# Memory attention and an eight-expert layer in one kernel: first weight splits one step earlier, one count later, and late pairs of blocks with a half-full second block

## The chip, the cores and the metric

The kernel runs on one core of one Trainium2 chip. A core has a matrix engine (TensorE, PE in the profile; its weight loads are shown as PEld), a vector engine (VectorE, DVE), a scalar engine (ScalarE, ACT), a general engine (GpSimd, POOL) and a queue engine that issues DMAs (SyncE, SP). Each engine takes its instructions in the order of the program; between engines, semaphores make one wait for another. Matrix products land in PSUM, which has eight banks of 128 x 512 float32; everything else lies in SBUF.

The metric is the device time of one execution in microseconds. Lower is better. The profile is one execution, taken by the hardware profiler; its span runs from the first to the last instruction.

## What is computed

Attention over 32 memory slots for 8 batches of 8 heads, and then a layer of eight experts in which each token goes to one expert:

```python
a = softmax(phi)                      # over 32 memory slots, phi: 8 x 8 x 576 x 32
k_m = einsum('bhsm,bhsd->bhmd', a, k) # memories, 32 x 64 per head
v_m = einsum('bhsm,bhsd->bhmd', a, v)
attn = softmax(q @ k_m^T / 8)
x = (attn @ v_m)                      # heads put side by side: 4608 tokens x 512
logits = x @ w_gate                   # 8 experts
e_idx = argmax(logits, axis=1)
for e in range(8):
    mask = e_idx == e
    h = relu(x[mask] @ w1[e])         # 512 -> 1024
    ye = h @ w2[e]                    # 1024 -> 512
    out[mask] = gate_w[mask] * sigmoid(x[mask] @ w_output_gate[:, e]) * ye
```

All inputs are float32. On the inputs that are drawn, the experts get 576, 576, 0, 0, 576, 1152, 1152 and 576 tokens, worked out from the reference. In blocks of 128 rows, 576 is four full blocks and one of 64 rows, and 1152 is nine full blocks.

## The kernel before

**Stages.** The first stage is attention for four pairs of batches (`bp`). For each, chunks of k and v and the softmax of phi become memories (`memory`), and then 5 steps of 1024 queries run through `scores`, `shift`, `expo`, `divide`, `back` and `values`; the rows x go to a DRAM table `xs` with their two gate factors behind them. After each pair of batches, `rank` finds each token's expert and its rank within the expert. The second stage is the expert layer, in slots of three blocks of 128 rows (a triple), two blocks (a pair), or one (a single), all of one expert. It starts before attention is over.

**Slots.** There are 5 early triples, which are filled from the first two and then three pairs of batches (`route_early`, lists `idx_a` and `idx_b`), and, once all tokens are known (`route_late`, list `idx_l`), 5 late triples, 4 pairs and up to 22 singles. Triples and pairs always run; the singles stand behind branches and run only if some are used. `route_late` forms the number of blocks left per expert, takes triples off it, makes a pair of two that remain, and a single of one.

**A slot.** Weights come as 8 tiles of 128 x 1024 float32 per slot (`Stream`): `fetch` issues the DMA on SP, `split` makes two parts of a tile, the rounded part with a cast on ACT (L564) and the rest with a subtraction on DVE (L565), in a tile `whl` with both. x and h are split the same way, and a product takes three matmuls, high by high, low by high and high by low (`PASS`). In `several`, the first four tiles (units u of 0 to 3) give h transposed: per unit two halves of 12 matmuls each (L1176), then ReLU into `hh` on ACT (L1181) and the remainder into `hl` on DVE (L1182). The second four tiles give y per block k: per unit and block two chunks f of three matmuls of 512 columns (L1198), with 128 x 128 of `hh` or `hl` as the loaded weights. `finish_y` scales y with the gate on ACT (L1155) and scatters the rows with an indirect DMA from POOL. In the last slot of a stream the turns (u, k) are sorted by k.

**x for the next slot.** While a slot's y runs, `nxt` prepares the next slot's x in four parts c of 0 to 3 (`turn_x`), at the turns that `TURN` lists. For early slots PE transposes (L1041). For the late ones that are gathered in quarters, DVE transposes `xg` into `xt` (L1035), ACT rounds it to `xh` (L1043) and DVE subtracts to `xl` (L1044); each such slot also has four small copies `gx` on ACT (L1031).

**Order.** The program is written out by Python generators. `ORDER` is the list of pieces of one attention step; each piece is one tick. "W" is the piece that splits the first two weight tiles, at step `START` = 17; the expert layer starts at piece "S" of that step. From there, `hook` runs at each half unit and each turn: it advances attention by three pieces and routing by two. `hold(n)` lets n ticks pass between a piece of routing that one engine does and the piece of another that needs it. `counts` is one small matmul that adds the counts `ohc` over the partitions (L278). `MEM` is the same kind of list for `memory`.

```python
def hold(n):
    if "open" not in env: return
    end = clock[0] + n
    while clock[0] < end: yield
```

The functions that the diff touches are printed here with the line numbers of the profile.

## Time and profile before

| | us |
|---|---|
| median of 3 runs | 578.09 (577.61 to 582.82) |
| the profiled execution | 577.36 |
| its span | 575.6 |
| PE busy | 529.1 (92%) |
| DVE busy | 356.1 (62%) |
| ACT busy | 280.4 (49%) |
| POOL busy | 229.2 (40%) |

A row of the timeline gives the start and the duration in microseconds, the engine, the line, the operation, what is written from what, shapes and count, and in brackets the time that the engine sat idle before it and what ended that. A row of a table of windows gives the stretch, its length, the busy time of each engine, the mean granted PE clock as a share of full speed, the share of the DMA engines that was busy, and GB/s. Rows of the timeline that are merged cover several instructions; matmuls overlap, so a row's duration is longer than the distance from one to the next.

### The profile page before, as it was taken

Reading aid. Unit: us, or ns where it says so; the run is one execution under the profiler, and the core shown is the slowest. Engines: PE = TensorE matmul, PEld = TensorE weight load, DVE = VectorE, ACT = ScalarE, POOL = GpSimd, SP = SyncE. Lnnn points to the kernel's source line nnn. Section 1 sums busy time; section 2 is a strip of 40 time slices with the busy share of each in tenths; the row PEclk is TensorE's granted clock in tenths of the full one; section 3 lists DMA queues with packets and bytes.
Section 4 is the critical chain, followed back from the end, with each engine's and each line's share of the span. In section 5 each row is a group of like instructions: output and inputs, shape, how many; then the busy total and the mean of one; then the engine's idle time right before and its main releaser. Section 6 shows DMA issues by size and latency. Waiting matters only on the chain. (4 is left out here: it accounts for less than half of the span.)

```text
span 575.6 us, 10886 instructions
## 1 busy us (share of the span) xinstructions
PE 529.1 (92%) x4031; PEld 455.6 (79%) x4031; DVE 356.1 (62%) x736; ACT 280.4 (49%) x496; POOL 229.2 (40%) x253
## 2 busy tenths in 40 slices
PE   3688886789899999999999999999999999999993
PEld 2455554478689799898998989898998989899893
DVE  4485979767765659996443555646465555676610
ACT  3475655454254456453434545445454445656510
POOL 2242575831166034312471735547170604553011
PEclk9987879989899999999999999999999999999998
DMA  8999999975367659756564665656465655687000
GB/s 308 413 401 391 382 376 356 308 301 168 116 197 245 209 173 308 246 155 183 161 200 145 204 177 180 184 171 176 139 202 168 179 172 181 198 264 223 7 28 32
DMA packets 42238, 124.14 MB, mean 216 GB/s; under 512 B 10368, under 2 KB 10432, under 8 KB 41792
## 3 DMA queue, kind: packets, MB, share of 16 engines
q1 hardware_dynamic: 35136, 102.71, 54.7%
q0 software_dynamic: 7040, 20.65, 10.4%
q8 instruction: 33, 0.54, 0.4%
q14 instruction: 29, 0.24, 0.1%
HBM read 102.99 MB, written 20.87 MB: 215 GB/s over the span
## 5 line engine op out<-in xcount | busy, mean ns | idle before, releaser
L1176 PE MATMUL bps<-xh,whl 128*128 128x384 f32 (+1 forms) x896 | 213.6, 322 | 0.1
L1198 PE MATMUL bps<-whl,hh 128*128 128x512 f32 x608 | 197.7, 396 | 0.0
L565 DVE TENSOR_TENSOR whl<-w,whl 128x1024 fp32r<-128x1024 f32 x112 | 136.8, 1228 | 68.5 <-ACT whl L564 68.5
L1176 PEld LDWEIGHTS bps<-xh,whl 128*128 128x128 f32 x896 | 156.9, 190 | 1.9 <-issue 0.6
L1176 PE MATMUL bps<-xl,whl 128*128 128x384 f32 (+1 forms) x448 | 143.8, 321 | 0.0
L1198 PEld LDWEIGHTS bps<-whl,hh 128*128 128x128 f32 x608 | 114.7, 189 | 26.1 <-issue 2.5
L1198 PE MATMUL bps<-whl,hl 128*128 128x512 f32 x304 | 119.0, 391 | 0.0
L564 ACT CAST whl<-w 128x1024 fp32r<-128x1024 f32 x112 | 116.4, 1046 | 0.0
L519 POOL DMA_INDIRECT xg<-xs,idx_ql x80 | 90.2, 1127 | 25.2 <-issue 24.3
L1181 ACT ACTIVATE hh<-bps 128x384 fp32r<-128x384 f32 (+1 forms) x96 | 48.9, 510 | 96.9 <-PE bps L1176 96.7
L1182 DVE SCALAR_TENSOR_TENSOR hl<-bps,hh 128x384 fp32r<-128x384 f32 (+1 forms) x96 | 55.1, 577 | 52.1 <-ACT hh L1181 52.1
L1176 PEld LDWEIGHTS bps<-xl,whl 128*128 128x128 f32 x448 | 85.1, 190 | 0.5
L1156 POOL DMA_INDIRECT out<-y,idx_ol x23 | 24.9, 1081 | 127.1 <-ACT y L1155 101.4
L1198 PEld LDWEIGHTS bps<-whl,hl 128*128 128x128 f32 x304 | 57.5, 189 | 10.8
L838 POOL TENSOR_TENSOR ea<-ea,mx 128x512 f32<-128x512 f32 (+1 forms) x20 | 19.2, 961 | 49.8 <-DVE mx L836 45.4
L1043 ACT CAST xh<-xt 128x384 fp32r<-128x384 f32 (+1 forms) x32 | 14.7, 460 | 37.9 <-DVE xt L1035 37.9
L873 ACT COPY xo<-bpd 128x576 f32<-128x576 f32 x36 | 22.6, 640 | 21.3 <-PE bpd L871 12.7
L956 POOL TENSOR_SCALAR Aw<-iota_row,row 128x128 bf16<-128x128 bf16 x36 | 26.8, 759 | 12.4 <-DVE row L946 12.4
L871 PE MATMUL bpd<-ve_b,aT 64*128 64x144 f32 (+1 forms) x320 | 28.5, 327 | 2.4 <-DVE ea L833 2.4
L1044 DVE TENSOR_TENSOR xl<-xt,xh 128x384 fp32r<-128x384 f32 (+1 forms) x32 | 15.8, 492 | 24.1 <-ACT xh L1043 24.1
L1155 ACT ACTIVATE y<-bps,gx 128x512 f32<-128x512 f32 x20 | 13.4, 687 | 30.4 <-PE bps L1198 13.9
L871 PEld LDWEIGHTS bpd<-ve_b,aT 64*128 64x128 f32 (+1 forms) x320 | 21.7, 196 | 8.1 <-issue 3.5
(248 smaller groups left out, 471.6 us busy)
## 6 DMA issues: line engine op xcount, KB each, us to landing
w<-wall SPq DMA_DIRECT2D x112, 512.0 KB, 3.9
kvt<-kv SPq DMA_DIRECT2D x32, 512.0 KB, 7.5
xs<-xo SPq DMA_DIRECT2D x16, 576.0 KB, 5.8
qt<-qT SPq DMA_DIRECT2D x16, 512.0 KB, 9.1
ph<-phiT SPq DMA_DIRECT2D x3, 1152.0 KB, 12.1
kv<-kv SPq DMA_DIRECT2D x4, 512.0 KB, 9.0
xg<-xs,idx_ql POOLq DMA_INDIRECT x80, 4.2
ph<-phiT SPq DMA_DIRECT2D x4, 288.0 KB, 3.2
```

Of the source, the lines that this page charges most:

```text
L519: G.indirect_dma_start(out=z["xg"][:, k, XQ * b:XQ * b + XQ], out_offset=None, in_=xs[0:z["rows"]].rearrange("t (a q) -> (t a) q", a=4), i ...
L564: A.copy(hl[:, 0], w[:])
L565: V.tensor_tensor(hl[:, 1], w[:], hl[:, 0].bitcast(F32), ALU.subtract)
L838: G.tensor_tensor(eav, eav, mx[:, 0:n].unsqueeze(2).to_broadcast([P, n, M]), ALU.subtract)
L871: T.matmul(px[to:to + n, r, sl], z["aT"][h, o:o + n], ves[2 * bp + b][h, g], start=True, stop=True)
L873: A.copy(xo[:, c % 2], px[:, :, 0:2 * XQ])
L956: (G if AWP else V).tensor_scalar(Aw[:, bp * NCH + c], iota_row[:], row[:, c:c + 1], None, ALU.is_equal)
L1156: G.indirect_dma_start(out=out, out_offset=bass.IndirectOffsetOnAxis(ap=z["idx"][1][:, z["q0"] + k:z["q0"] + k + 1], axis=0), in_=y[:], in ...
L1176: T.matmul(pb[:, j % pb.shape[1], 0:n_], w[:, b, o:o + P], x[a][:, cc, 0:n_], start=(n == 0), stop=(n == 11))
L1181: A.activation(h_[:, js, 0:n_], pb[:, :, 0:n_], AF.Relu)
L1182: V.scalar_tensor_tensor(l_[:, js, 0:n_], pb[:, :, 0:n_], 0.0, h_[:, js, 0:n_].bitcast(F32), ALU.max, ALU.subtract)
L1198: T.matmul(py[k], h[u - 4][a][:, f, k * P:(k + 1) * P], w[:, b, DM * f:DM * f + DM], start=(u == 4 and f == 0 and n == 0), stop=(u == 7 an ...
```

## The change

It has four parts.

1. "W" stands behind the second "M" of a step in place of ahead of "X", and acts at step `START - 1`, so that the first two splits come ahead of the growth of the pools, too. One entry of `MEM` changes places with an empty one.
2. The DMA of `wg` is issued after the four DMAs of the first `phi`.
3. In `route_early` the wait ahead of `counts` is twice as long. Early routing ahead of the expert layer doesn't wait at all (`hold` returns), so this bears on the second early list alone.
4. A late pair is made only where the expert's last block holds at most 64 rows (`odd`, from the count of half blocks); otherwise its two blocks become singles. In a pair, `hh` holds both parts of h in one tile of 384 columns: block 0 high (0 to 127), block 1 high (128 to 191), block 1 low (192 to 255), block 0 low (256 to 383). For block 1, the 128 columns from 128 on are loaded as one set of weights, and two matmuls, by the high and by the low part of w2, give the product of the high part of h in PSUM partitions 0 to 63 and that of the low part in 64 to 127. `finish_y` adds the halves with a copy on ACT and an addition on DVE, and scales and scatters 64 rows. In the last slot, block 1 goes first.

```diff
-ORDER = ["R4", "W", "X", "S", "R0", "m", "D", "M", "B", "V0", "R1", "R1", "V1", "M", "m", "C"]
+ORDER = ["R4", "X", "S", "R0", "m", "D", "M", "B", "V0", "R1", "R1", "V1", "M", "W", "m", "C"]
...
-        nc.sync.dma_start(wg[64:128], wgo)
...
-            yield from hold(LATE["pe"])
+            yield from hold(2 * LATE["pe"])
             n_ = counts(k + 1)
...
+            V.tensor_scalar(odd[:], n_, 63.0, None, ALU.add)
...
+            V.tensor_scalar(odd[:], odd[:], 6, 1, ALU.arith_shift_right, ALU.bitwise_and)
...
             V.tensor_scalar(ti[:, 1], ti[:, 2], 2.0, 2.0, ALU.is_ge, ALU.mult)
+            yield
+            V.tensor_tensor(ti[:, 1], ti[:, 1], odd[:], ALU.mult)
...
             load_phi(0)
+            nc.sync.dma_start(wg[64:128], wgo)
...
-                        while t == START and stream.split(2):
+                        while t == START - 1 and stream.split(2):
...
-            A.activation(y[:], py, AF.Copy, scale=z["g"][:, k:k + 1] if z["quart"] else z["xg"][:, k, P:P + 1])
+            n = P
+            if (z["nb"], k) == (2, 1):
+                n = 64
+                ya = env["xt"].tile([64, DM], F32, name="ya", bufs=1)
+                A.copy(ya[:], py[64:128])
+                V.tensor_tensor(ya[:], py[0:64], ya[:], ALU.add)
+                py = ya[:]
+            A.activation(y[0:n], py[0:n], AF.Copy, scale=...)
...
-                l_ = mo.tile([P, 2, 3 * P], F32R, name="hl", bufs=4)
+                l_ = mo.tile([P, 2, 3 * P], F32R, name="hl", bufs=4) if nb == 3 else None
...
+                    elif j == 1:
+                        A.activation(h_[:, :, 0:192], pb[:, :, 0:192], AF.Relu)
+                        for o, c, m in ((192, P, 64), (256, 0, P)):
+                            V.scalar_tensor_tensor(h_[:, :, o:o + m], pb[:, :, c:c + m], 0.0,
+                                                   h_[:, :, c:c + m].bitcast(F32), ALU.max, ALU.subtract)
...
-                turns.sort(key=lambda t: t[1])
+                turns.sort(key=lambda t: t[1], reverse=nb == 2)
...
+                    elif k == 0:
+                        ps = [(h_[:, f, 256 * a:256 * a + P], b) for a, b in PASS]
+                    else:
+                        ps = [(h_[:, f, P:256], b) for b in range(2)]
```

Three places show how instructions move. In these rows the line numbers of the changed kernel differ from those before: L277 is `counts`, L1224 the y matmul, L831 `scores`, L877 `values`, L1047 the transpose of x, L570 and L569 the two halves of a split, L1050 `xl`. `bps` and `bpd` are PSUM banks, `pr` the one of routing.

The first is PE in the y of slot 0, around `counts` for the second early list (`ohc_91`). Before:

```order
L871 MATMUL bpd<-ve_b,aT 128x144 x4
L278 LDWEIGHTS ones_b
L278 MATMUL pr<-ohc_91,ones_b 128x8
L1198 MATMUL bps<-whl,hh 128x512
L1198 MATMUL bps<-whl,hl 128x512
L1198 MATMUL bps<-whl,hh 128x512 x2
L1198 MATMUL bps<-whl,hl 128x512
L1198 MATMUL bps<-whl,hh 128x512
L825 MATMUL bpd<-qt,kT_203 32x64 x8
L825 MATMUL bpd<-qt,kT_204 32x64 x8
L1041 MATMUL bps<-ident,xg 128x128 x3
```

And changed:

```order
L877 MATMUL bpd<-ve_b,aT 128x144 x4
L1224 MATMUL bps<-whl,hh 128x512
L1224 MATMUL bps<-whl,hl 128x512
L1224 MATMUL bps<-whl,hh 128x512 x2
L1224 MATMUL bps<-whl,hl 128x512
L1224 MATMUL bps<-whl,hh 128x512
L831 MATMUL bpd<-qt,kT_202 32x64 x8
L831 MATMUL bpd<-qt,kT_203 32x64 x8
L277 LDWEIGHTS ones_b
L277 MATMUL pr<-ohc_91,ones_b 128x8
L1047 MATMUL bps<-ident,xg 128x128 x3
```

The small matmul has moved behind the six y matmuls of one turn and the two groups of `scores`, to just ahead of the transposes of x. (`kT` is one of four buffers; its number says nothing here.)

The second is DVE around the first two splits. Before:

```order
L858 STREAM_TRANSPOSE aT<-ea 128x256
L779 COPY ve_b<-bpa 128x2x16
L565 TENSOR_TENSOR whl<-w,whl 128x1024 x2
L833 STREAM_TRANSPOSE ea<-bpd 128x512
L836 TENSOR_REDUCE mx<-ea 128x16
```

And changed:

```order
L864 STREAM_TRANSPOSE aT<-ea 128x256
L570 TENSOR_TENSOR whl<-w,whl 128x1024 x2
L785 COPY ve_b<-bpa 128x2x16
L839 STREAM_TRANSPOSE ea<-bpd 128x512
L842 TENSOR_REDUCE mx<-ea 128x16
```

The copy of the gate columns `ve_b` has moved behind the two splits; the order on ACT, where the casts stand, has not changed there.

The third is ACT in the y of a pair that another pair follows. Before:

```order
L1031 COPY gx<-xg 32x2 x4
L1043 CAST xh<-xt 128x256
L564 CAST whl<-w 128x1024
L1043 CAST xh<-xt 128x256
L564 CAST whl<-w 128x1024
L1043 CAST xh<-xt 128x256 x2
L564 CAST whl<-w 128x1024
L1155 ACTIVATE y<-bps,gx 128x512 x2
L564 CAST whl<-w 128x1024
L1181 ACTIVATE hh<-bps 128x2x256
```

And changed:

```order
L1037 COPY gx<-xg 32x2 x4
L1049 CAST xh<-xt 128x256
L569 CAST whl<-w 128x1024
L1049 CAST xh<-xt 128x256
L569 CAST whl<-w 128x1024
L1049 CAST xh<-xt 128x256 x2
L569 CAST whl<-w 128x1024
L1169 ACTIVATE y<-bps,gx 128x512
L1166 COPY ya<-bps 64x512
L1169 ACTIVATE y<-ya,gx 64x512
L569 CAST whl<-w 128x1024
L1199 ACTIVATE hh<-bps 128x2x192
```

The two new instructions of block 1 stand behind all casts of the next pair's x and ahead of the next pair's first `hh`; the casts of weights between them are unchanged in number.

## The prediction

> **What bounds the kernel now.** I read the page's slices first, then the table of windows, the waits, and the timeline of PE at the changed places.

> ```profile
> span 575.6 us, 10886 instructions
> PE   3688886789899999999999999999999999999993
> PEclk9987879989899999999999999999999999999998
> 100.00:150.00 50.00, 41.11 (x432) 32.96 (x433) 35.79 (x79) 22.79 (x44) 20.59 (x25) 0.90 0.73 247
> 150.00:560.00 410.00, 410.00 (x2326) 370.05 (x2325) 250.05 (x450) 200.08 (x322) 163.07 (x150) 1.00 0.59 180
> ```

> From 150 to 560 us PE is busy in every microsecond and at full clock; DVE and ACT have 250 and 200 us of work in these 410. So there a matmul removed is time gained, as long as what feeds PE keeps up; and an idle gap ahead of 150 us counts in full if nothing closes up behind it. The changed parts lie in two places: the last 40 us before 150, and the four pairs, the last slots that run. The median before is 578.09; the profiled execution took 577.36, 0.7 less, and the sum is made against 577.36. Its 1.8 us around the span, and the end (last matmul, `y`, scatter, landing), stay: the last block finished is again one of 128 rows.

> That pairs stay pairs at all follows from the reference: the experts with two blocks left have 576 tokens, 4 x 128 + 64, so `odd` is 1 for each.

> **The later count.**

> ```profile
> 142.77 0.53 PE L871 MATMUL bpd<-ve_b,aT 64*128 64x144 f32 x6
> 145.46 0.16 DVE L913 TENSOR_TENSOR ohc<-ohc,oc 128x8 bf16<-128x8 bf16 x1
> 145.68 0.17 PE L278 MATMUL pr<-ohc,ones_b 128*128 128x8 bf16 x1 [2.37 <-DVE ohc L913]
> 145.70 0.47 PE L1198 MATMUL bps<-whl,hh 128*128 128x512 f32 x1
> 147.32 0.68 PE L825 MATMUL bpd<-qt,kT 64*32 64x64 f32 x32
> 147.93 0.90 PE L1041 MATMUL bps<-ident,xg 128*128 128x128 f32 x3
> 148.48 0.78 PE L1198 MATMUL bps<-whl,hh 128*128 128x512 f32 x1
> 150.90 0.21 PE L924 MATMUL pr<-ohg,strict 128*128 128x72 bf16 x1
> 147.40:150.30 2.90, 2.90 (x39) 0.50 0.88 316
> ```

> PE ends its work at 142.77 + 0.53 = 143.30, stands 2.37 us for `ohc`, and then runs at half clock from 147.4 to 150.3. In the changed order the six y matmuls (145.70 to 147.32, 1.62) and `scores` (147.32 to 147.93, 0.61) come first: 143.30 + 1.62 + 0.61 = 145.53, and `counts` at 145.68 hardly waits. The transposes start at 145.70 in place of 147.93: 2.23 gained. If the half clock is due to the gap, it goes too. The transposes and six matmuls took 150.90 - 147.93 = 2.97; at full clock

> ```profile
> 262.16 0.51 PE L1041 MATMUL bps<-ident,xg 128*128 128x128 f32 x3
> 262.43 0.48 PE L1198 MATMUL bps<-whl,hh 128*128 128x512 f32 x1
> 148.87 0.48 ACT L1043 CAST xh<-bps 128x384 fp32r<-128x384 f32 x1 [4.87 <-PE bps L1041]
> 149.38 0.56 DVE L1044 TENSOR_TENSOR xl<-bps,xh 128x384 fp32r<-128x384 f32 x1 [2.94 <-ACT xh L1043]
> 149.85 0.44 DVE L833 STREAM_TRANSPOSE ea<-bpd 128x256 f32<-128x256 f32 x1
> 150.66 0.37 DVE L990 TENSOR_REDUCE lg<-xo 128x32 f32<-128x128 f32 x1
> ```

> they take 0.27 + 6 x 0.23 = 1.65: another 1.3. What is late next: the rank matmul (L924) needs the same PSUM tile `pr`, which is free when DVE has read the counts, and that read now stands behind `xl`, `ea`, `mx` and `lg`. From the start of the transposes to the cast was 0.94, and I take 0.75 at full clock (an estimate: the three transposes themselves shrink from 0.55 to 0.27, less the part that is latency), then by these rows 0.51 to `xl`, 0.47 to `ea`, 0.81 to `lg`, 0.3 and 0.3 for the read: 145.70 + 3.1 = 148.8, plus 0.1. PE is there after 0.27 + 12 x 0.23 = 3.05, at 148.75. So 0.15 comes back. Term: -(2.23 + 1.3) + 0.15 = -3.4; ends 0 (a new stall as long as the old) and -3.5.

> [...]

> **The first split.**

> ```profile
> 114.68 0.19 DVE L779 COPY ve_b<-bpa 128x32 f32<-128x32 f32 x1 [0.95 <-PE bpa L774]
> 115.93 2.36 DVE L565 TENSOR_TENSOR whl<-w,whl 128x1024 fp32r<-128x1024 f32 x2 [1.05 <-ACT whl L564]
> 118.20 0.71 DVE L833 STREAM_TRANSPOSE ea<-bpd 128x512 f32<-128x512 f32 x1
> 118.97 1.41 PE L1041 MATMUL bps<-ident,xg 128*128 128x128 f32 x9 [1.87 <-DVE ea L833]
> ```

> The splits wait for their casts on ACT, whose order is the same, so they come no earlier. `ve_b` now runs behind them, ahead of `ea`, for which PE waits to have its banks: +0.15. The first weight DMAs after the splits use other buffers; their order on SP is the same, and the split that needs them comes after the first two units of h. The `MEM` entry moves within a step between pieces without work on these engines: 0. The `wg` DMA:

> ```profile
> 0.80 0.59 SPq L159 DMA_DIRECT2D wg<-wgo  x1
> 6.42 0.11 DVE L155 MEMSET upto<- 128x64 f32 x1
> 6.45 2.67 DVE L677 TENSOR_REDUCE nmx<-ph 128x1 f32<-128x576 f32 x4
> ```

> `phi` is issued 0.6 earlier, but DVE takes it up right after its own setup at 6.42: 0. The three small DVE steps for `odd`, and the routing steps that they push back by a hook, lie in the stretch where PE is always busy: 0; were that cover gone, some 0.2 us each. Scores that move a tick sit between matmuls: 0.

> **The pairs.** In the y of a pair 8 of 48 matmuls of 512 columns go. The second pair's y starts and ends, and the eleventh matmul of the third pair's h starts, in these rows:

> ```profile
> 511.05 0.40 PE L1198 MATMUL bps<-whl,hh 128*128 128x512 f32 x1
> 521.96 0.28 PE L1176 MATMUL bps<-xh,whl 128*128 128x256 f32 x1
> 523.15 0.28 PE L1176 MATMUL bps<-xl,whl 128*128 128x256 f32 x1
> ```

> The 48 take 521.96 - 511.05 = 10.91, 0.227 each; 8 are 1.82 and four pairs 7.27. But the next pair's x has to be ready when y ends:

> ```profile
> 511.31 0.60 ACT L1181 ACTIVATE hh<-bps 128x512 fp32r<-128x512 f32 x1 [1.34 <-PE bps L1176]
> 511.94 0.69 DVE L1182 SCALAR_TENSOR_TENSOR hl<-bps,hh 128x512 fp32r<-128x512 f32 x1 [0.72 <-ACT hh L1181]
> 512.88 1.23 DVE L565 TENSOR_TENSOR whl<-w,whl 128x1024 fp32r<-128x1024 f32 x1 [0.24 <-ACT whl L564]
> 514.02 0.44 DVE L1035 STREAM_TRANSPOSE xt<-xg 128x256 f32<-128x256 f32 x1
> 517.50 0.41 ACT L1043 CAST xh<-xt 128x256 fp32r<-128x256 f32 x1 [1.65 <-DVE xt L1035]
> 517.82 1.05 ACT L564 CAST whl<-w 128x1024 fp32r<-128x1024 f32 x1
> 518.90 1.23 DVE L565 TENSOR_TENSOR whl<-w,whl 128x1024 fp32r<-128x1024 f32 x1 [0.53 <-ACT whl L564]
> 521.77 0.41 ACT L1043 CAST xh<-xt 128x256 fp32r<-128x256 f32 x1 [0.85 <-DVE xt L1035]
> 522.21 0.43 DVE L1044 TENSOR_TENSOR xl<-xt,xh 128x256 fp32r<-128x256 f32 x1 [0.47 <-ACT xh L1043]
> ```

> From the last `hh` on, ACT and DVE wait only for each other: DVE transposes, ACT rounds and casts a weight tile, DVE subtracts and splits that tile, and so on. The chain starts when h ends (511.05) and its last `xl` ends at 522.64, 11.59 later, however fast PE is. The matmul that needs it is the eleventh of the next h, at 523.15: half a microsecond of slack. With 40 matmuls y ends after 9.09, and the eleventh would start at 9.09 + 1.19 = 10.28. The chain begins some 0.1 sooner (`hh` has 384 columns for 512 that take 0.60: an estimate), and PE's wait for a semaphore takes about as long: ready at 11.56. So PE stalls about 1.28, and 1.82 - 1.28 = 0.54 is left. This holds between pairs 1 and 2, 2 and 3, and 3 and 4; behind the fourth no x follows, and the 1.82 is whole. Term: -(3 x 0.54 + 1.82) = -3.4; ends -1.8 (each transition gives all back) and -7.3 (no stall).

> New work: per unit two DVE subtractions (128 and 256 elements) for one of 512, per pair an ACT copy and a DVE addition of 64 x 512. The rows above have 0.60 on ACT and 0.69 on DVE for 128x512, and no row has 64 partitions; I take these, and half of them as the lower end. They stand behind the next pair's x and run beside its first h, which lasts 96 x 0.119 = 11.4 us (ten matmuls from 521.96 to 523.15); the scaling waits on ACT for the addition, the next `hh` behind it is late by some 1.5 us, and that is caught up by the third unit. In the last pair block 1 comes first and needs the last `hh` after 12 matmuls, 2.7 us; by the rows above it takes 0.26 + 0.5 + 0.8 = 1.6. Cost 0.

> **Sum.** 577.36 - 3.4 + 0.15 - 3.4 = 570.7.

> **The rivals.**
> - The x chain doesn't bind, as when ACT and DVE in fact pace themselves by PE: 577.36 - 3.25 - 7.27 = 566.8. For it: PE now never waits there. Against it: the brackets in the rows above name only ACT and DVE.
> - The stall for `counts` comes back at L924 or behind it, by a DVE queue that runs later than I reckon: 577.36 + 0.15 - 3.4 = 574.1. For it: only 0.15 between the two; against it: DVE is fed by the earlier transposes.
> - The half clock stays although the gap goes: 570.7 + 1.3 = 572.0. [...]
> - Slower: the scaling that waits on ACT holds up the next `hh` and casts so that the next chain starts late, by d per transition. The gain of 6.7 is lost when 3 d exceeds it, d over 2.2 us; at d = 4, 577.36 - 6.7 + 12 = 582.7. Against it: ACT has in a pair 8 casts of 1.05, 4 of `hh`, 4 of `xh` 4 of `gx` and 3 more, about 15 of some 22 us.

> **How the numbers follow.** My forecast has 0.52, its own range 569 to 572.5 (0.5 on each of the two large terms, and the 0.7 between this execution and the median); no chain 0.13; the counts' stall back 0.13; half clock 0.12; slower 0.04; and 0.06 for smaller gains by several of these at once. The predicted time is that of the likeliest, 570.7. The range reaches to both outer rivals, 566.5 to 574.3: it holds the forecast, the clock's rival and somewhat more than half of each of the outer two, whose centres lie at its bounds, about 8 in 10. A measurement tells about 1% from no change, 5.8 us of 578.09, so below 572.3 is faster: 0.42 of the forecast's 0.52, all of the first rival and part of the clock's, 0.6 in all; slower is 0.04, and the same 0.36.

> **What would show it.** PE idle ahead of `counts` under 0.4 us and clock 1.0 between 146 and 150; PE waits of together 1.3 us for `xh` and `xl` at the start of pairs 2, 3 and 4, and 40 matmuls of 9.1 us in each pair's y; no wait in the last one. Wrong would be: no PE wait at the pairs, a wait at L924 over 1 us, or singles in the trace.

## The result, and the profile after

The changed kernel takes 570.92 us (median of 4 runs, 569.47 to 572.79), the kernel before 578.33 beside it (4 runs, 577.61 to 582.82): a ratio of 0.986, 95% interval 0.983 to 0.990, or 7.4 us less. The profiled execution of after took 570.68 and spans 569.0 us.

The page of after, two rows of its table of slices, and three stretches by engine (length, then busy us and instructions of PE, PEld, DVE, ACT and POOL, the granted clock, the share of DMA time, GB/s):

```profile
span 569.0 us, 10851 instructions
PE   3688766689999999999999999999999999999993
PEclk9979789979999999999999999999999999999998
...
143.00:145.60 2.60, 2.48 (x46) 1.73 (x45) 2.57 (x5) 0.64 (x1) 0.59 (x1) 1.00 0.00 0
145.90:150.00 4.10, 4.10 (x29) 3.34 (x29) 3.02 (x8) 2.06 (x4) 0.62 (x1) 1.00 0.77 197
150.00:560.00 410.00, 408.68 (x2301) 367.66 (x2300) 247.72 (x470) 199.70 (x326) 163.31 (x150) 1.00 0.59 181
```

The hole ahead of 146 us is closed and the clock behind it is 1.00. Behind 150 us PE is still busy nearly all the time, but no longer in every microsecond: 410.00 less 408.68 is 1.3 us of waiting that was not there before. These 1.3 us are a lower bound of what is lost, since the rows of matmuls become longer while PE waits (0.38 us where the same row takes 0.28, below).

PE around `counts`, in the timeline (start, length, then the operation, its tiles and its count; in brackets the idle time before it and what ended that), behind two rows of before with the matmuls of attention's values:

```profile
142.55 0.76 PE L871 MATMUL bpd<-ve_b,aT 64*128 64x144 f32 x8
154.11 0.76 PE L871 MATMUL bpd<-ve_b,aT 64*128 64x144 f32 x8
...
142.75 0.76 PE L877 MATMUL bpd<-ve_b,aT 64*128 64x144 f32 x8
145.03 0.45 PE L831 MATMUL bpd<-qt,kT 64*32 64x64 f32 x32
145.87 0.17 PE L277 MATMUL pr<-ohc,ones_b 128*128 128x8 bf16 x1 [0.39 <-DVE ohc L919]
145.89 0.53 PE L1047 MATMUL bps<-ident,xg 128*128 128x128 f32 x3
149.01 0.21 PE L930 MATMUL pr<-ohg,strict 128*128 128x72 bf16 x1
150.83 0.76 PE L877 MATMUL bpd<-ve_b,aT 64*128 64x144 f32 x8
```

In after, `counts` waits 0.39 us where it waited 2.37. The rank matmul (L930) has no bracket: the wait did not come back there. The matmuls of attention's values that follow, the last row, stood at 154.11 before and stand at 150.83 now, 3.28 earlier. From the same product ahead of the count (142.55 before, 142.75 now) it is 8.08 us where it was 11.56, so this stretch gained 3.48.

The waits of PE and of its weight loads after 151 us (in all, times, longest), and the transition from the second to the third pair on PE, ACT and DVE (the row of L1181 is of before):

```profile
PE bps L1191 <- ACT xh L1049: 0.9, 3, 0.3
PEld bps L1191 <- DVE xl L1050: 1.6, 6, 0.3
PEld bps L1191 <- ACT xh L1049: 1.5, 3, 0.5
...
507.15 9.26 PE L1224 MATMUL bps<-whl,hh 128*128 128x512 f32 x40
516.24 0.28 PE L1191 MATMUL bps<-xh,whl 128*128 128x256 f32 x1
518.20 0.38 PE L1191 MATMUL bps<-xh,whl 128*128 128x256 f32 x1 [0.29 <-ACT xh L1049]
...
507.41 0.49 ACT L1199 ACTIVATE hh<-bps 128x384 fp32r<-128x384 f32 x1 [1.45 <-PE bps L1191]
529.34 0.49 ACT L1199 ACTIVATE hh<-bps 128x384 fp32r<-128x384 f32 x1 [1.45 <-PE bps L1191]
533.73 0.60 ACT L1181 ACTIVATE hh<-bps 128x512 fp32r<-128x512 f32 x1 [1.35 <-PE bps L1176]
...
518.18 0.42 DVE L1050 TENSOR_TENSOR xl<-xt,xh 128x256 fp32r<-128x256 f32 x1 [0.47 <-ACT xh L1049]
```

y starts at 507.15 and its 40 matmuls are through at 516.24, after 9.09. The last quarter of the next pair's x is ready only at 518.18 + 0.42 = 518.60, 11.45 after y began, and each of three transitions shows PE or its weight loads waiting for `xh` and `xl`. From one pair's last `hh` to the next pair's is 529.34 - 507.41 = 21.93; before it was 533.73 - 511.31 = 22.42. In after it is 21.93 at all three transitions. Eight matmuls fewer, 1.82 us of work, bring 0.49.

### The profile page after: what moved, and what is told of

Read it like the earlier page. It is cut to its first block, busy times and chain, and to the rows that moved or that the text cites. A ratio compares the mean times of both kernels' runs of the same rounds, so it can differ in the third digit from the quotient of the medians.

```text
span 569.0 us, 10851 instructions
## 1 busy us (share of the span) xinstructions
PE 520.7 (92%) x3999; PEld 448.4 (79%) x3999; DVE 356.9 (63%) x759; ACT 280.3 (49%) x500; POOL 229.2 (40%) x253
## 5 line engine op out<-in xcount | busy, mean ns | idle before, releaser
L1224 PE MATMUL bps<-whl,hh 128*128 128x512 f32 x640 | 193.9, 394 | 0.0
L570 DVE TENSOR_TENSOR whl<-w,whl 128x1024 fp32r<-128x1024 f32 x112 | 136.6, 1225 | 75.6 <-ACT whl L569 75.5
L1224 PEld LDWEIGHTS bps<-whl,hh 128*128 128x128 f32 x640 | 119.9, 188 | 24.8 <-issue 0.2
L569 ACT CAST whl<-w 128x1024 fp32r<-128x1024 f32 x112 | 116.1, 1044 | 0.0
L524 POOL DMA_INDIRECT xg<-xs,idx_ql x80 | 91.5, 1143 | 25.3 <-issue 24.4
L1224 PE MATMUL bps<-whl,hl 128*128 128x512 f32 x240 | 93.7, 390 | 0.0
L1170 POOL DMA_INDIRECT out<-y,idx_ol x23 | 26.1, 1135 | 121.7 <-ACT y L1169 95.2
L1195 ACT ACTIVATE hh<-bps 128x384 fp32r<-128x384 f32 x80 | 39.0, 493 | 71.7 <-PE bps L1191 71.7
L1196 DVE SCALAR_TENSOR_TENSOR hl<-bps,hh 128x384 fp32r<-128x384 f32 x80 | 43.9, 553 | 35.7 <-ACT hh L1195 35.6
L1224 PEld LDWEIGHTS bps<-whl,hl 128*128 128x128 f32 x240 | 45.1, 188 | 8.4
L1050 DVE TENSOR_TENSOR xl<-xt,xh 128x384 fp32r<-128x384 f32 (+1 forms) x32 | 15.7, 492 | 24.2 <-ACT xh L1049 24.2
L1169 ACT ACTIVATE y<-bps,xg 128x512 f32<-128x512 f32 x18 | 12.4, 689 | 36.5 <-PE bps L1224 10.0
L877 PE MATMUL bpd<-ve_b,aT 64*128 64x144 f32 (+1 forms) x320 | 27.6, 320 | 2.5 <-DVE ea L839 2.4
L877 PEld LDWEIGHTS bpd<-ve_b,aT 64*128 64x128 f32 (+1 forms) x320 | 20.9, 190 | 8.4 <-issue 3.1
```

The source lines that it names most:

```text
L524: G.indirect_dma_start(out=z["xg"][:, k, XQ * b:XQ * b + XQ], out_offset=None, in_=xs[0:z["rows"]].rearrange("t (a q) -> (t a) q", a=4), i ...
L569: A.copy(hl[:, 0], w[:])
L570: V.tensor_tensor(hl[:, 1], w[:], hl[:, 0].bitcast(F32), ALU.subtract)
L877: T.matmul(px[to:to + n, r, sl], z["aT"][h, o:o + n], ves[2 * bp + b][h, g], start=True, stop=True)
L1170: G.indirect_dma_start(out=out, out_offset=bass.IndirectOffsetOnAxis(ap=z["idx"][1][0:n, z["q0"] + k:z["q0"] + k + 1], axis=0), in_=y[0:n] ...
L1195: A.activation(h_[:, j], pb[:, 0], AF.Relu)
```

## The experiments

Each row is the median; the ratio is to the kernel before, run on the same chip.

| kernel | us | ratio, 95% interval |
|---|---|---|
| before with the later count alone | 576.17 | 0.995 (0.993 to 0.997) |
| before with the new pairs alone | 574.45 | 0.993 (0.991 to 0.995) |
| after, next x prepared from y's first turn | 567.21 | 0.979 (0.978 to 0.981) |
| before, next x prepared from y's first turn | 579.3 | 1.001 (0.999 to 1.002) |
| after, count two turns earlier | 577.73 | 0.998 (0.997 to 0.999) |
| after without the earlier split and the moved load | 572.46 | 0.989 (0.986 to 0.991) |
| the third row's kernel without those two, twice | 568.75 and 567.94 | 0.982 (0.980 to 0.984) and 0.982 (0.979 to 0.985) |
| the third row's kernel with the load alone back at its old place | 568.16 | 0.981 (0.978 to 0.984) |
| the third row's kernel with the split alone back at its old place | 567.24 | 0.979 (0.976 to 0.982) |
| the third row's kernel again | 567.42 | 0.980 (0.978 to 0.983) |

**The later count alone.**

```diff
-            yield from hold(LATE["pe"])
+            yield from hold(2 * LATE["pe"])
```

> The kernel before with the longer wait ahead of counts alone. Theory (the changed kernel gains 3.3 us by the count, half clock included, and 3.3 us by the pairs): 3.3 to 3.6 us less than before, about 574.7 of 578.1; PE waits under 0.6 us for ohc and its clock is 1.0 from 146 to 150 us; the pairs as before. Rival A (the pairs give their full 7.3 us and the count nothing): no change, 578. Rival B (the half clock has nothing to do with the gap): 2.0 to 2.3 us less, and a clock of 0.5 somewhere between 145 and 152 us.

It took 576.17, 2.5 less than before's 578.67 there, so between the theory and the rival without the clock; the interval, 2.0 to 4.2 less, holds both. The trace decides between them. Its PE around the count, and the first matmul of h in this execution and in before's:

```profile
147.88 0.17 PE L278 MATMUL pr<-ohc,ones_b 128*128 128x8 bf16 x1 [0.40 <-DVE ohc L913]
151.01 0.21 PE L924 MATMUL pr<-ohg,strict 128*128 128x72 bf16 x1
...
122.40 0.67 PE L1176 MATMUL bps<-xh,whl 128*128 128x384 f32 x1
...
120.43 0.69 PE L1176 MATMUL bps<-xh,whl 128*128 128x384 f32 x1
```

The wait is gone, and the clock is 1.00 from 140 to 160 us: the half clock that the rival needs is not there. But the stretch up to the first h, which is the same here, ended 2.0 us later than in the profiled execution of before. From the first h to the end of the span it is 574.4 - 122.40 = 452.0 against 575.6 - 120.43 = 455.2: 3.2 less, near the 3.4 expected. So single executions have to be compared from the first h on, and the medians carry that spread as noise.

**The new pairs alone** (before, with the fourth part of the change and nothing else).

> The changed kernel with only its fourth part (pairs with a half-full second block, both parts of h in one load); the first splits, the place of wg and the wait ahead of counts are as before. Theory (the next pair's x is late after the shorter y): 3 x 0.5 + 1.85 = 3.3 us less than before, about 574.8 of 578.1; PE waits at the start of the second, third and fourth pair, the first three parts' stretch as before with a wait of 2.4 us for ohc. Rival A (full gain of 32 matmuls): 7.3 us less, 570.8. Rival C (the new work on ACT and DVE takes all back): no change.

It took 574.45, 4.2 less (interval 3.1 to 5.3): the bound without a stall, 570.8, falls. The waits for `xh` and `xl` behind 151 us are those of after, row for row. From the matmuls of attention's values at 154 us, which stand alike in both (154.06, and 154.11 before), to the start of the last y on ACT (563.72 for 567.04) it gains 3.3. Its count still waits 2.36 us, and yet its clock stays at 1.00; this is taken up below.

**The next x from the first turn.** The pair's y takes four weight tiles; behind which of its eight turns a quarter of the next x is asked for is a table.

```diff
-TURN = {3: (1, 4, 6, 9), 2: (1, 2, 4, 5)}
+TURN = {3: (1, 4, 6, 9), 2: (0, 1, 2, 3)}
```

> The changed kernel with the next pair's x prepared at turns 0, 1, 2 and 3 of a pair's y in place of 1, 2, 4 and 5, so that one split of weights less stands within the chain of DVE and ACT. Theory: the chain from the end of h to the last xl shrinks by about 1.75 us, from 11.45 to 9.7 us, under the 10.3 at which PE needs it; no PE wait between pairs, each of three transitions gains 1.3 us more, 4.0 us in all: 566.9 where the changed kernel has 570.9. Rival (the waits between pairs have another cause, such as the copy and the addition at the end of a pair): the waits stay, 570.9.

> The kernel before with the same turns 0, 1, 2 and 3 in a pair's y. Theory: before the change y was long enough and x half a microsecond early, so there is nothing to gain: 578.1, within 0.5 us. Rival (earlier x helps a pair whatever the length of its y, since DVE or ACT limit it): 3 to 4 us less.

On after it took 567.21, 3.7 less where 4.0 was expected; on before it changed nothing that can be measured (579.3 against 578.67). In the changed kernel PE then has no wait left after 151 us. The same transition:

```profile
506.26 9.26 PE L1224 MATMUL bps<-whl,hh 128*128 128x512 f32 x40
515.36 0.28 PE L1191 MATMUL bps<-xh,whl 128*128 128x256 f32 x1
...
506.53 0.49 ACT L1199 ACTIVATE hh<-bps 128x384 fp32r<-128x384 f32 x1 [1.45 <-PE bps L1191]
527.13 0.49 ACT L1199 ACTIVATE hh<-bps 128x384 fp32r<-128x384 f32 x1 [1.45 <-PE bps L1191]
...
515.55 0.43 DVE L1050 TENSOR_TENSOR xl<-xt,xh 128x256 fp32r<-128x256 f32 x1 [0.47 <-ACT xh L1049]
```

The last `xl` ends at 515.98, 9.72 after y began, as two weight tiles are now prepared behind it. The period is 527.13 - 506.53 = 20.60, and 22.42 - 20.60 is the whole 1.82 of eight matmuls. This settles the stall: it is the order of ACT's and DVE's work, since the same work in another order has none, and it cost nothing before because y was longer. This version is faster than both.

**The count two turns earlier.**

```diff
-            yield from hold(2 * LATE["pe"])
+            yield from hold(0)
```

> The changed kernel with the count asked for two turns earlier (no hold at all instead of a doubled one), so one turn earlier than before the change. What the count waits for is made by DVE and does not move, so PE, done at about 141.0 in the profile of before's clock of time, waits until 145.6: a gap of about 4.6 us in place of 0.39, +4.2. My theory, that a gap ahead of the transposes brings a half clock behind it: a stretch of 2.5 to 3.4 us at 0.5, +1.3 to 1.7 more; in all 576.5 to 577 beside 570.9. Rival, the half clock has nothing to do with the gap: clock 1.0 behind it, 575.1. Rival, an earlier count lets later routing work come earlier and so pays back: under 573.

It took 577.73, 6.8 more than after and 0.7 above the 576.5 to 577 expected. The gap is 4.64 us, 4.25 longer than after's. The rest is a clock that stayed at half for two stretches, not one: the next experiment's table has the rows.

**A second profile of before.**

> The kernel before, unchanged, for a second profiled execution. Question: is the half clock behind the 2.37 us gap there each time? Theory A, a gap of this length halves the clock always: 0.5 for about 2.9 us behind the count. Theory B, it depends on where the gap lies in some fixed beat, since one kernel with a gap of 2.36 showed 1.0 all through and another with 2.35 showed 0.5: then either may be seen here, and the term of 1.3 us is worth 1.3 only in a share of executions. The first h matmul comes anywhere between 120 and 125 us, and the time from it to the end of the span is 455.2, or 453.9 without a half clock.

It showed the half clock again, 0.50 from 149.3 to 152.6, and from its first h to its end 577.7 - 122.67 = 455.0 (580.05 in this one run). Four executions have a gap of 2.35 to 2.37 us ahead of the count: two of before, one of before with the earlier x, and one of the pairs alone. Read in windows of 0.1 us, the clock of the first profile changes at 113.1, 116.5, 119.9, 123.3, 147.2 and 150.6, all multiples of 3.41 us apart (to 0.1 us); the second profile has its half clock over 3.4 us again, but 2.1 us off these places. Two stretches of about that length for each, from the one that holds most of the gap (stretch, length, PE's busy time and matmuls, granted clock, DMA share, GB/s). Before, before again, before with the earlier x, pairs alone, and last three stretches of the count two turns earlier:

```profile
143.80:147.10 3.30, 1.42 (x7) 1.00 0.26 25
147.20:150.50 3.30, 3.30 (x41) 0.50 0.82 296
...
145.90:149.20 3.30, 1.38 (x7) 1.00 0.25 22
149.30:152.60 3.30, 3.30 (x41) 0.50 0.84 295
...
146.20:149.50 3.30, 0.94 (x11) 1.00 0.00 0
149.60:153.00 3.40, 3.40 (x41) 0.50 0.87 218
...
145.40:148.70 3.30, 1.60 (x11) 1.00 0.31 24
148.80:152.10 3.30, 3.30 (x55) 1.00 0.85 305
...
142.10:145.40 3.30, 0.47 (x8) 1.00 0.33 129
145.50:148.80 3.30, 1.60 (x5) 0.50 0.24 35
148.90:152.20 3.30, 3.30 (x13) 0.50 0.31 122
```

A stretch with PE idle for 1.9 us or more (3.30 less 1.42, 1.38, 0.94 or 0.47) is followed by one at half clock; one with 1.7 idle was followed by full clock in the pairs alone and, already at half clock, by a second half one in the count two turns earlier. So theory A is out, since behind a gap of 2.35 to 2.37 us the clock was half in three of these four executions and full in the fourth, and theory B fits: in the three, 1.9 us or more of PE idling fell into one stretch, in the fourth 1.7. Put to the whole profiles of before and of after, in steps of 3.41 us from 14.0 us on: of the 307 steps at full clock, all 291 with up to 1.33 us of PE idling were followed by full clock and all 13 with 1.72 or more by half clock; of the three between, the one with 1.41 was followed by half clock and those with 1.46 and 1.50 by full clock. Of the 17 steps at half clock, the three with 0.91 us of idling or more were followed by another one at half clock, and two of the 14 with 0.39 or less. That also closes the account of the count two turns earlier: 4.25 of gap, and from 147.2 to 152.3 about 5.1 us at half clock, worth 2.5, make 6.8.

**The split and the load.** First both undone, on after and on the version with the earlier x, then each alone, with two controls.

```diff
-ORDER = ["R4", "X", "S", "R0", "m", "D", "M", "B", "V0", "R1", "R1", "V1", "M", "W", "m", "C"]
+ORDER = ["R4", "W", "X", "S", "R0", "m", "D", "M", "B", "V0", "R1", "R1", "V1", "M", "m", "C"]
...
-                        while t == START - 1 and stream.split(2):
+                        while t == START and stream.split(2):
...
         wg = cp.tile([P, H, 16], F32, name="wg")
+        nc.sync.dma_start(wg[64:128], wgo)
...
             load_phi(0)
-            nc.sync.dma_start(wg[64:128], wgo)
```

> The changed kernel without the earlier first split and without the moved load of the gate's weights (and with the old list of loads). My sum gave the split +0.15 us and the load 0; so without them 570.7, no difference that can be measured. Rival, the earlier split or load is worth something that the profile of one execution hides, since the stretch up to the first h differs by over 4 us between executions of one and the same front: then 572 or above, or, if they cost, 569 or below.

> The same with the next pair's x prepared from the first turn on (the quickest version so far, 567.21, with both parts undone). My theory: 567.0, within 0.5 of the version that has them. Rival: over 568.2, the two parts save 1 us or more in the stretch before the first h; or under 566.2, they cost it.

> The version with the earlier x chain (567.21) with the load of the gate's weights put back to the front of its queue, all else as there. Undoing load and split together gave 568.75, 1.5 more. In the traces the kernels without the two parts reach the last transposed attention weights before the split at 113.3 to 116.7 us (seven executions, mean 114.8), those with them at 113.3 to 113.6 (three); the split comes after that. So my theory now: the load carries the 1.5, here 568.4 to 569. Rival, the split carries it: 567.2 here. Rival, neither, the spread of the front: all four kernels of this call within 0.7.

> The same version with the first split put back to the later place, the load as changed. If the load carries the 1.5: 567.0 to 567.2 (my sum has the split at +0.15). If the split carries it, by bringing the first weight loads forward or in another way: 568.4 to 569.

> The version with both parts again, as the control on this chip: 567.2 as before if the chip and the day make no difference.

> The version without both parts again, as the other control: 568.75 as before if the 1.5 between the two is real; 567.2 if it was chance.

Undone on after they gave 572.46, on the other version 568.75: 1.5 more each time, which was the rival's outcome and not the expected one, and the second control only 0.5 more (567.94 against 567.42). With the load alone at its old place it took 568.16, with the split alone at its old place 567.24. Put together, 17 runs of the version with the earlier x with the load at the front of its queue have a mean of 568.4, 16 runs with it behind `phi` 567.3: 1.1 less, 95% interval 0.4 to 1.8. These come from three chips; on the one that ran all four kernels, 12 runs each, it is 0.9 (0.0 to 1.7), and with the earlier split the time there is 0.1 less (-0.9 to 1.1). The runs alone would leave doubt, since a single pair of these kernels doesn't separate. The traces show what the load does. The first 8 and the first 20 us (columns as in the first fence) of before and of the version with the load at its old place, then of after and of the second control:

```profile
0.00:8.00 8.00, 0.00 (x0) 0.00 (x0) 4.73 (x29) 2.31 (x5) 3.68 (x23) 1.00 0.67 222
0.00:20.00 20.00, 10.15 (x155) 7.02 (x159) 7.47 (x34) 8.87 (x21) 4.29 (x24) 1.00 0.88 336
...
0.00:8.00 8.00, 0.00 (x0) 0.00 (x0) 4.74 (x29) 2.32 (x5) 3.68 (x23) 1.00 0.66 218
0.00:20.00 20.00, 10.22 (x132) 7.03 (x133) 6.34 (x33) 8.26 (x20) 4.29 (x24) 1.00 0.88 333
...
0.00:8.00 8.00, 0.00 (x0) 0.00 (x0) 4.74 (x29) 2.32 (x5) 3.68 (x23) 1.00 0.78 262
0.00:20.00 20.00, 10.20 (x159) 7.02 (x163) 7.49 (x34) 8.85 (x21) 4.29 (x24) 1.00 0.93 351
...
0.00:8.00 8.00, 0.00 (x0) 0.00 (x0) 4.74 (x29) 2.32 (x5) 3.68 (x23) 1.00 0.77 271
0.00:20.00 20.00, 10.22 (x132) 7.10 (x133) 6.37 (x33) 8.27 (x20) 4.29 (x24) 1.00 0.92 354
```

With the load behind `phi`, 351 to 358 GB/s were moved in the first 20 us in all five executions that have it so, and 328 to 337 in all nine that don't; about 22 GB/s in 20 us is 0.45 MB, which takes 1.2 us at the 383 GB/s that after reaches from 20 to 100 us. DMA is busy all that while (share 1.01 there), so what starts sooner ends sooner: the eighth transpose of the attention weights `aT` on DVE comes at 71.6 to 72.0 us in the five and at 72.1 to 75.2 in the nine. So the load carries it. At the first h, some 50 us later, the two groups overlap (120.81 to 122.39 for the five, 120.43 to 124.74 for the nine, means 0.8 apart), so its size in the whole time rests on the runs above. The moved entry in `MEM` moves no instruction on any engine. The split carries nothing that can be measured, to within about 1 us.

## Why the prediction was right, and where it was not

The predicted 570.7 is within 0.3 us of the median, and the range held it. By its own steps:

- **Later count, the gap: right.** Foreseen were no more than 0.4 us of waiting ahead of `counts`, 2.23 gained, and 0.15 lost at L924. It was 0.39, 1.98 less than 2.37. Counted from the matmuls of `values` ahead of the count (142.55 and 142.75), the transposes come 5.38 - 3.14 = 2.24 earlier; the rest of that is the end of the stretch, which before ran at half clock from 147.2 on. At L924 nothing was lost. The rival in which the stall comes back there is out.
- **Later count, the half clock: right in mechanism, wrong as a fixed term.** The 1.3 went into the sum whole, once the half clock was seen in one profile. It is there in three of four executions with the gap, so about 1.0 on average, and none of the nine executions with a gap of 0.39 or 0.40 has it (1.00 from 140 to 160 us in each). The rival in which the half clock stays although the gap goes is out, since it went with the gap.
- **The first split: right**, as far as it can be seen. `ve_b` does run behind the splits; in after PE waits 2.23 for `ea` where it waited 1.87. The time shows neither gain nor loss.
- **The load of the gate's weights: the step that failed.** The prediction had "`phi` is issued 0.6 earlier, but DVE takes it up right after its own setup at 6.42: 0". That is true of `phi`'s first user, and it was the wrong user to ask. Behind `phi` in the same queue stand the transfers for attention, and DMA is busy up to 100 us (in after a share of 0.93 in the first 20 us and of 1.01 from there on); the 0.6 us went to them. It is worth 1.1 us (0.4 to 1.8). Why it is more than 0.6 is not shown; while `wg` leads the queue, from 2 to 3 us, DMA moves 74 GB/s at a share of 0.58, and after moves 226 at 0.76 in the same microsecond.
- **The pairs: right in mechanism and size.** Foreseen was an x ready 11.56 after y begins, a stall of 1.28 at three transitions, 0.54 left of each 1.82, and all of it behind the fourth pair. Measured were 11.45, a stall of 21.93 - 20.60 = 1.33, and 0.49 left. PE's wait for a semaphore, which the prediction put at about 0.1, is 0.06 here: the last `xl` ends at 518.60, and its matmul starts at 518.66. The sign that was named, 1.3 us of PE waiting for `xh` and `xl` at each start, does not show at that size: PE's rows have 0.9 in all for the three, and the rest stands in the waits of its weight loads and in longer rows. The copy and the addition took 0.59 and 0.68 us and stand, as foreseen, behind the next x; ACT waits for PE again at the third `hh` of the pair. The rival without a chain (566.8) is out, and so is the slow one, in which the scaling holds up the next chain.

Put together from what was measured: 2.0 for the gap, about 1.0 for the clock, 3.3 for the pairs (three times 0.49 and once 1.82) and 1.1 for the load are 7.4, and 578.33 - 570.92 is 7.4. Each of these is known to a few tenths at best, so that they add up exactly is chance. The prediction had 6.7 and started from an execution that was 0.7 below the median it knew and is 1.0 below the one measured beside after. That it came within 0.3 us is therefore luck in part: the load that it left out is about as large as what it had too much for the clock and that start together.

## What to carry to other kernels

When an engine that bounds a stage gets less work, look for the next chain that runs beside it and at the order in which that chain does its pieces; here asking for the quarters of the preparation one or two turns earlier, in a table, brought 3.7 us that removing matmuls alone did not. When a transfer is moved in a queue, ask what every later transfer of that queue feeds, not only the next one, and cost it by the DMA share of the whole stage behind it. Before a term is built on a clock seen at half once, check in a second execution whether it is there.

## What was not expected of the hardware

The stretch up to the first h differs between executions by up to 4.3 us with the same order of instructions (120.43 to 124.74), more than most parts of this change are worth. What spreads it was not found out.
